# Columns of w1 read 36 apart, h laid out by nine transposes, and a finer last piece of wo in a decode kernel

## The chip, the cores and the metric

The kernel runs on one core of a Trainium2 chip. The metric is the device time of one execution in microseconds (us), as the median of several runs. The kernel before takes about 1295.3 us, and its fast runs lie between 1294.6 and 1297.3 us, so a difference of less than about 2 us means little in a single run.

The engines are TensorE (PE in the profile; PEld is its weight loads), VectorE (DVE), ScalarE (ACT), GpSimd (POOL) and SyncE (SP), which issues the loads here. The 16 DMA engines move data between HBM, the chip's main memory, and SBUF, the core's working memory.

A few words recur. A matmul takes two operands from SBUF: `lhsT`, loaded first as weights, and `rhs`, the *moving operand*; it writes to PSUM, TensorE's output memory. An *eviction* copies a result from PSUM to SBUF. A load is *issued* when SyncE puts it into the queue and *lands* when its completion is signalled. A *group* is, for the caches, one of 32 parts of K and V, and, in the up phase below, six matmuls that add up to one block of h. The *granted clock* is the share of full speed at which TensorE was allowed to run.

## The reference, cut to what matters

```python
B, D, H, Sk, Dh, F = 8, 576, 32, 4096, 128, 4608
def reference(...):
    x = A_x
    g = sigmoid((x * gate_w).sum(-1, keepdims=True))
    # A: one query per sequence against a cache of 4096 keys in each of 32 heads
    q = (x @ wq) -> [B, H, 1, Dh]
    a = softmax(q . k_cache * Dh**-0.5) @ v_cache -> @ wo
    # B: a small MLP on the layernormed x
    h = gelu(layernorm(x) @ w1 + b1)         # [8, 576] @ [576, 4608]
    b = h @ w2 + b2                          # [8, 4608] @ [4608, 576]
    return g * a + (1 - g) * b
```

The two caches are 2 x 8 x 32 x 4096 x 128 bf16 numbers, 537 MB. All weights together are 20 MB. All of it is read once.

## The kernel before

SBUF holds three big slots of 64 KB per partition. All loads of weights and caches are issued by SyncE into one queue, in a fixed order, each into the slot of the load three places earlier: wq, w1 and w2 first, then K of group 0 (called k0), k1, v0, k2, v1, k3 and so on over 32 groups. A load of 8.4 MB may be issued only when its slot is free. So k1 waits for the last matmul that reads w1, v0 for the last one that reads w2, k2 until k0 is worked off, and v1 until k1 is worked off.

```python
free[0] = [p_Q]               # k0 waits for the last read of wq
...
free[1] = [p_up]              # k1 waits for the last "up" matmul (reads w1)
...
free[2] = [p_b2]              # v0 waits for the last "down" matmul (reads w2)
```

The up phase computes h in four quarters of F (index c), each on its own quarter of TensorE's output columns (PSUM partitions 32c and up), in three blocks of 384 columns (index k). A group of six matmuls makes one block of one quarter: five over the rows of w1, and a sixth of a single row that adds the bias.

```python
for k in range(3):
    for c in range(4):
        col = c * FC + k * FB                       # FC = 1152, FB = 384
        o = up_ps[32 * c:32 * c + B, k, 0:FB]
        for kt in range(NKT):                       # 5
            r = w1_sb[:, kt, col:col + FB] ...      # 384 neighbouring columns
            p_up = op("tensor", lambda e, ...: e.matmul(o, lhsT=yT_sb[:, yi, :], rhs=r, ...))
        p_up = op("tensor", lambda e, ...: e.matmul(
            o, lhsT=one1[:, :], rhs=b1_row[:, col:col + FB], start=False, stop=True))
... gelu on VectorE and ScalarE into hrow [4 quarters x 8, 1152] ...
for j in range(NJ):                                 # 36 transposes of 32 columns, 36 apart
    p_hT = op("tensor", lambda e, j=j: e.matmul(
        ht_ps[0:32, j, :, :], lhsT=hrow[0:QP, j::NJ], rhs=per_quarter, ...))
v_hT = [op("vector", lambda e, c=c: e.tensor_copy(  # four evictions
    out=hT_sb[32 * c:32 * c + 32, :, :], in_=ht_ps[0:32, :, c, :]), [p_hT]) for c in range(4)]
```

w2 lies in SBUF with rows 36p to 36p+35 on partition p, so the transposed h must have row 36p + j on partition p too. That is where the step of 36 comes from.

At the end wo arrives in three pieces of rows, 32 x 4 small matmuls add it in, four evictions fill `out_sb`, and one store writes the result.

## Time and profile before

| | before |
|---|---|
| median of 3 runs | 1295.32 us (1294.81 to 1297.27) |
| bytes moved | 557.16 MB at a mean of 431 GB/s |
| busy share of the big load queue | 99.6% |
| TensorE / VectorE busy | 57% / 63% |
| up phase (first up matmul to the issue of k1) | 27.3 to 43.0 us |

Part 2 of the page of the kernel before cuts the span into 40 slices of 32.3 us. PEclk is TensorE's granted clock in tenths, DMA the busy share of the DMA engines in tenths, GB/s what they moved.

```profile
PEclk8799898878898887898787899778888877888888
DMA  9999999999999999999999999999999999999998
GB/s 406 427 447 424 439 430 436 432 430 436 434 428 436 436 432 438 430 438 432 430 436 434 428 436 438 430 438 430 438 430 432 436 432 434 432 438 430 436 424 366
DMA packets 10591, 557.16 MB, mean 431 GB/s; under 512 B 1201, under 2 KB 1233, under 8 KB 1745
```

The DMA engines are busy from the first slice to the last at a nearly constant rate. The kernel is bound by its loads: an engine can only cost time if it makes the queue run empty.

The timeline of SyncE before shows when loads were issued (start us, length us, engine, line, what, count). Its first line here merges two loads: k0 at 20.62 and k1 at 42.96.

```profile
20.62 22.68 SPq L384 DMA_DIRECT2D SL<-in_A_k_cache_dram  x2
59.34 0.33 SPq L384 DMA_DIRECT2D SL<-in_A_v_cache_dram  x1
84.42 0.33 SPq L384 DMA_DIRECT2D SL<-in_A_k_cache_dram  x1
111.47 0.33 SPq L384 DMA_DIRECT2D SL<-in_A_v_cache_dram  x1
```

The records of the same trace give the landings: k0 59.8, k1 79.2, v0 98.6, k2 117.9, v1 137.3 us. With the queue full a load lands every 19.35 us.

The timeline of TensorE in the up phase (start, length, line, operation, output and inputs, shape, count), at full clock:

```profile
31.30 0.98 PE L515 MATMUL PS<-SL 128*8 128x384 bf16 x5
32.20 0.32 PE L518 MATMUL PS<-SL,one 1*8 1x384 bf16 x1
32.45 0.98 PE L515 MATMUL PS<-SL 128*8 128x384 bf16 x5
33.36 0.32 PE L518 MATMUL PS<-SL,one 1*8 1x384 bf16 x1
```

Groups of six follow each other every 1.15 us. The windows view sums the engines and gives the clock (columns: stretch, length, busy time and count of PE, PEld, DVE, ACT, POOL, then clock, DMA share, GB/s). The first two groups ran at half clock:

```profile
27.30:31.30 4.00, 3.96 (x13) 1.14 (x13) 0.00 (x0) 0.00 (x0) 0.00 (x0) 0.55 1.15 498
31.30:43.00 11.70, 11.63 (x61) 4.29 (x60) 0.03 (x1) 0.00 (x0) 0.00 (x0) 1.00 0.97 419
```

The transposes of h and their evictions, and the last 3 us of the kernel, in the timeline:

```profile
50.60 2.30 PE L535 MATMUL PS<-ident,SL 104*32 104x32 bf16 x36 [7.67 <-DVE SL L528]
52.94 1.89 DVE L538 CAST SL<-PS 32x288 bf16<-32x288 f32 x4 [2.39 <-PE PS L535]
...
1290.22 0.30 PE L544 MATMUL PS<-SL,OT 128*8 128x144 bf16 x8 [0.21 <-DMA SL<-in_A_wo_dram]
1290.57 0.57 ACT L761 CAST out_sb<-PS 8x144 bf16<-8x144 f32 x2 [5.70 <-PE PS L544]
1290.57 0.63 DVE L761 CAST out_sb<-PS 8x144 bf16<-8x144 f32 x2 [3.50 <-PE PS L544]
1291.23 0.37 SPq L326 DMA_DIRECT2D out_dram<-out_sb  x1
```

### The profile page before, as it was taken

The numbers are of one execution on the slowest core, as the hardware profiler recorded it, in microseconds if no ns is written. First come the engines' busy times: TensorE is split into PE (matmuls) and PEld (weight loads), VectorE is DVE, ScalarE is ACT, GpSimd is POOL, SyncE is SP. The second block draws the span as 40 slices with busy tenths as digits, with TensorE's granted clock in tenths as the row PEclk, the third lists the DMA queues.
The fourth block names the chain that finished last, engine by engine and source line by source line (L and its number), as shares of the span: only waits on it lengthen the run. The fifth ranks groups of instructions, "written<-read, shape, count | busy, mean of one in ns | idle before, by whom it ended". The sixth has DMA issues, their size and how long they took to land.

```text
span 1293.2 us, 11790 instructions
## 1 busy us (share of the span) xinstructions
PE 733.4 (57%) x4926; PEld 337.1 (26%) x4926; DVE 819.7 (63%) x873; ACT 161.0 (12%) x587; POOL 40.4 (3%) x60
## 2 busy tenths in 40 slices
PE   3666566555556555556555556555556555556646
PEld 1322223122223222223222223222223222223223
DVE  2387567665567665567665567765567765567762
ACT  1011110111110011110011110011111011111011
POOL 1001000000000000000000000000000000000000
PEclk8799898878898887898787899778888877888888
DMA  9999999999999999999999999999999999999998
GB/s 406 427 447 424 439 430 436 432 430 436 434 428 436 436 432 438 430 438 432 430 436 434 428 436 438 430 438 430 438 430 432 436 432 434 432 438 430 436 424 366
DMA packets 10591, 557.16 MB, mean 431 GB/s; under 512 B 1201, under 2 KB 1233, under 8 KB 1745
## 3 DMA queue, kind: packets, MB, share of 16 engines
q1 hardware_dynamic: 10528, 556.94, 99.6%
q8 instruction: 9, 0.15, 0.0%
q10 hardware_dynamic: 50, 0.04, 0.0%
q14 instruction: 4, 0.03, 0.0%
HBM read 556.96 MB, written 0.01 MB: 431 GB/s over the span
## 4 chain that ended last, share of the span: by engine, by line
DMA 54%; DVE 26%; PE 14%; ACT 5%; issue 1%; SPq 0%; ACTq 0%; DVEq 0%
DMA SL<-in_A_k_cache_dram 50%; DVE SL L580 20%; PE PS L585 7%; DVE s_sb L591 5%; ACT P L625 4%; PE PS L640 4%; DMA SL<-in_B_w_dram 2%; DMA SL<-in_A_wo_dram 2%; PE PS L515 1%; PE PS L656 1%; ACT O_sb L645 1%; PE PS L544 0%; PE PS L518 0%; PE PS L649 0%; PE PS L535 0%
## 5 line engine op out<-in xcount | busy, mean ns | idle before, releaser
L585 PE MATMUL PS<-SL,ident 128*128 128x512 bf16 x2048 | 547.7, 420 | 518.3 <-DVE SL L580 518.3
L580 DVE TENSOR_TENSOR SL<-SL,q_bc 128x4096 bf16<-128x4096 bf16 x256 | 582.0, 2284 | 313.6 <-DMA SL<-in_A_k_cache_dram 313.6
L585 PEld LDWEIGHTS PS<-SL,ident 128*128 128x128 bf16 x2048 | 199.0, 106 | 853.8 <-DVE SL L580 614.8
L591 DVE TENSOR_REDUCE s_sb<-PS 128x32 f32<-128x512 f32 x256 | 175.8, 687 | 90.4 <-PE PS L585 90.3
L625 ACT ACTIVATE P<-s_sb,hb 128x256 bf16<-128x256 f32 x256 | 126.2, 494 | 663.3 <-PE PS L640 645.5
L640 PE MATMUL PS<-SL,P 128*32 128x512 bf16 x2048 | 128.5, 389 | 0.0
L640 PEld LDWEIGHTS PS<-SL,P 128*32 128x32 bf16 x2048 | 96.4, 138 | 17.9 <-issue 3.1
L564 POOL TENSOR_SCALAR Qm<-Q,sel 128x256 bf16<-128x256 bf16 x33 | 33.7, 1020 | 896.6 <-ACT O_sb L645 845.2
L572 ACT ACTIVATE q_bc<-PS 128x128 bf16<-128x128 f32 x33 | 9.1, 277 | 407.4 <-PE PS L569 407.4
L625 ACT ACTIVATION_READ_ACCUMULATOR P<-s_sb,hb 128x1 f32 x256 | 47.7, 186 | 0.0
L656 PE MATMUL PS<-O_sb,selq 128*32 128x128 f32 x256 | 34.2, 278 | 0.7 <-ACT O_sb L645 0.7
L656 PEld LDWEIGHTS PS<-O_sb,selq 128*32 128x32 f32 x256 | 26.0, 113 | 1.4 <-ACT O_sb L645 1.2
L645 ACT ACTIVATE O_sb<-PS 128x512 f32<-128x512 f32 x32 | 18.4, 574 | 10.0 <-PE PS L640 10.0
L523 DVE COPY SL<-PS 104x1152 f32<-104x1152 f32 x1 | 1.4, 1357 | 28.7 <-PE PS L518 28.7
L515 PE MATMUL PS<-SL 128*8 128x384 bf16 x60 | 13.2, 356 | 6.8 <-DMA SL<-in_B_w_dram 6.8
L669 DVE SCALAR_TENSOR_TENSOR On<-PS,rz,dqm 32x128 f32<-32x128 f32 x32 | 10.9, 339 | 9.0 <-PE PS L656 7.9
L683 POOL TENSOR_TENSOR OT<-OTs,g 32x96 bf16<-32x96 f32 (+2 forms) x12 | 4.2, 347 | 320.3 <-DVE OTs L673 320.2
L610 DVE TENSOR_REDUCE mA<-s_sb 128x1 f32<-128x256 f32 x32 | 13.4, 420 | 1.1
L673 DVE TENSOR_REDUCE OTs<-On 32x32 f32<-32x128 f32 x32 | 12.1, 378 | 1.1
L649 PE MATMUL PS<-acc,hsel 128*32 128x8 f32 x64 | 7.4, 188 | 5.9 <-ACT O_sb L645 4.7
L663 DVE TENSOR_REDUCE zs<-PS 32x1 f32<-32x8 f32 x32 | 4.7, 147 | 8.2 <-PE PS L656 7.9
L649 PEld LDWEIGHTS PS<-acc,hsel 128*32 128x32 f32 x64 | 4.5, 110 | 19.5 <-issue 12.7
(82 smaller groups left out, 114.5 us busy)
## 6 DMA issues: line engine op xcount, KB each, us to landing
SL<-in_A_v_cache_dram SPq DMA_DIRECT2D x2, 4096.0 KB, 38.4
SL<-in_B_w_dram SPq DMA_DIRECT2D x1, 5184.0 KB, 37.7
SL<-in_B_w_dram SPq DMA_DIRECT2D x1, 4608.0 KB, 24.1
SL<-in_A_wq_dram SPq DMA_DIRECT2D x1, 4096.0 KB, 13.0
SL<-in_A_wo_dram SPq DMA_DIRECT2D x1, 3456.0 KB, 22.0
SL<-in_A_wo_dram SPq DMA_DIRECT2D x1, 864.0 KB, 23.7
SL<-in_B_w_dram SPq DMA_DIRECT2D x1, 576.0 KB, 25.0
SL<-in_A_wq_dram SPq DMA_DIRECT2D x1, 512.0 KB, 13.6
```

Of the source, the lines that this page charges most:

```text
L515: p_up = op("tensor", lambda e, o=o, r=r, kt=kt, yi=yi: e.matmul(o, lhsT=yT_sb[:, yi, :], rhs=r, start=(kt == 0), stop=False), [v_yT, *ld_ ...
L564: g_qm[g] = op("gpsimd", lambda e: e.tensor_scalar(out=Qm[:, :, :].rearrange("p k d -> p (k d)"), in0=Q4[:, 2 * hg * DH:(2 * hg + 2) * DH] ...
L580: v_mult[g, c] = op("vector", lambda e: e.tensor_tensor(out=part, in0=part, in1=qb, op=ALU.mult), [land["k", g], a_qb[g]], token="tensor" ...
L585: p_sum[g, c] = op("tensor", lambda e, r=r, n=n: e.matmul(tr_ps[par][:, :], lhsT=ident[:, :], rhs=r, start=(n == 0), stop=(n == NCH - 1)), ...
L591: v_red[g, c] = op("vector", lambda e: e.tensor_reduce(out=s_sb[:, c * CT:(c + 1) * CT], in_=tr_ps[par][:, :].rearrange("p (t c) -> p t c" ...
L610: t = op("vector", lambda e: e.tensor_reduce(out=mA[:, 0:1], in_=s_sb[:, :], axis=AX.X, op=ALU.max), [v_red[g, NCK - 1], c_mA], token=own)
L625: a_exp[g] = op("scalar", lambda e, h=h: e.activation(out=P[:, :, h, :], in_=s_sb[:, :].rearrange("p (s t) -> p s t", s=2), func=ACT.Exp, ...
L640: p_pv[g] = op("tensor", lambda e, o=o, lhsT=lhsT, rhs=rhs, tq=tq: e.matmul(o, lhsT=lhsT, rhs=rhs, start=(tq < 4), stop=(tq >= NTQ - 4)), ...
L645: a_ev[g] = op("scalar", lambda e: e.activation(out=O_sb[:].rearrange("p t d -> p (t d)"), in_=o_ps[:, :], func=ACT.Copy), [p_pv[g], p_z.g ...
L649: p_z[g] = op("tensor", lambda e: e.matmul(oz_ps[0:32, DH:DH + HB], lhsT=hsel[:, :], rhs=acc[:, place(g), :], start=True, stop=True), [a_e ...
L656: p_oz[g] = op("tensor", lambda e, tt=tt: e.matmul(oz_ps[0:32, 0:DH], lhsT=selq[:, tt, :], rhs=O_sb[:, tt, :], start=(tt == 0), stop=(tt = ...
L673: v_norm[g] = op("vector", lambda e: e.tensor_reduce(out=OTs[:, :, place(g + 2)], in_=On[:, :].rearrange("p (q j) -> p j q", q=NDQ), axis= ...
```

## The change

Its intent: if the up matmuls already take their columns 36 apart, h comes out in the order that the transposes want. Each transpose can then cover 128 columns in a row, nine do instead of 36, and one eviction does instead of four. The last row of wo arrives in two half-width pieces, so that half of the output can be evicted while the other half still arrives. One VectorE instruction leaves each softmax. Small copies at the start move from VectorE to ScalarE.

```diff
+    def columns(t, at):
+        return bass.AP(tensor=t.tensor, offset=t.offset + at, ap=[list(t.ap[0]), [1, 3], [NJ, 128]])
+
     for k in range(3):
         for c in range(4):
-            col = c * FC + k * FB
             o = up_ps[32 * c:32 * c + B, k, 0:FB]
+            at = c * NJQ + 3 * k
             for kt in range(NKT):
-                r = w1_sb[:, kt, col:col + FB] if kt < NKF else w1_t[...]
...
+                if kt < NKF:
+                    ks = [(w1_sb[:, kt, :], at, yT_sb[:, kt, :], o)]
+                else:                                     # the last rows: two matmuls of 192 columns
+                    ks = [(w1_t, at, yT_sb[:, NKF, :], 0), (w1_t, at, yT_sb[:, NKF + 1, :], 1)]
...
             p_up = op("tensor", lambda e, o=o, at=at: e.matmul(
-                o, lhsT=one1[:, :], rhs=b1_row[:, col:col + FB], start=False, stop=True), [ld_b1, c_one1])
+                o, lhsT=one1[:, :], rhs=columns(b1_row, at), start=False, stop=True), [ld_b1, c_one1])
...
-    for j in range(NJ):
-        p_hT = ... matmul(ht_ps[0:32, j, :, :], lhsT=hrow[0:QP, j::NJ], rhs=per_quarter, ...)
-    v_hT = [... tensor_copy(out=hT_sb[32 * c:32 * c + 32, :, :], in_=ht_ps[0:32, :, c, :]) ... for c in range(4)]
+    for i in range(NJQ):                                  # NJQ = 9
+        p_hT = ... matmul(ht_ps[:, i, :, :], lhsT=hrow[0:QP, i, :], rhs=per_quarter, ...)
+    v_hT = [... tensor_copy(out=hT_sb.rearrange("p (c i) b -> p i c b", c=4), in_=ht_ps)]
...  (softmax: the negation goes into the instruction that makes hb8; one tensor_scalar less)
-    WO = ((0, 24), (24, 30), (30, 32))
+    WO = ((0, 24, 0, 4), (24, 31, 0, 4), (31, 32, 2, 4), (31, 32, 0, 2))
...
+        for i in range(4) if j < NJO - 1 else (2, 3, 0, 1):
...  (each eviction waits for its own quarter alone; VectorE and ScalarE take turns)
```

More of the change, by code (lines that the diff above doesn't have):

```diff
@@ L36 @@
 FC = F // 4
+NJQ = NJ // 4
 FB = FC // 3
@@ L265, in bass_gated_mix__mha_block_cached__mixer_channel_mlp__decode_kernel @@
     b1_row = late.take([1, F])
-    hrow = late.take([128, FC])
+    hrow = late.take([128, NJ // 4, 128])
     hT_sb = late.take([128, NJ, B])
@@ L276, in bass_gated_mix__mha_block_cached__mixer_channel_mlp__decode_kernel @@
     zs = sb("zs", [32, 1], F32)
+    rz = sb("rz", [32, 1], F32)
     acc = sb("acc", [128, GL, HB], F32)
@@ L292, in bass_gated_mix__mha_block_cached__mixer_channel_mlp__decode_kernel @@
     ident = sb("ident", [128, 128], BF16)
-    hneg = sb("hneg", [128, HB], F32)
+    hpos = sb("hpos", [128, HB], F32)
     sel32 = sb("sel32", [128, HB, TQ], F32)
@@ L298, in bass_gated_mix__mha_block_cached__mixer_channel_mlp__decode_kernel @@
     mB = sb("mB", [128, 32], F32)
-    mC = sb("mC", [128, 32], F32)
     mD = sb("mD", [128, 32], F32)
@@ L304, in bass_gated_mix__mha_block_cached__mixer_channel_mlp__decode_kernel @@
     O_sb = sb("O_sb", [128, TQ, DH], F32)
-    rz = sb("rz", [128, 1], F32)
     PS = nc.alloc_psum_tensor("PS", [128, 8 * 512], F32)
@@ L317, in bass_gated_mix__mha_block_cached__mixer_channel_mlp__decode_kernel @@
     g32_ps = bank[3][0:32, 64:64 + 2 * B]
-    ht_ps = PS[:, 0:NJ * 32].rearrange("p (j c b) -> p j c b", j=NJ, c=4)
+    ht_ps = PS[:, 0:NJ * B].rearrange("p (i c b) -> p i c b", i=NJQ, c=4)
     xt_ps = bank[7]
@@ L405, in bass_gated_mix__mha_block_cached__mixer_channel_mlp__decode_kernel @@
                                                     base=PH - 1, pattern=[[PH, HB], [0, NDQ]], channel_multiplier=-1), [t])
-    c_hneg = op("vector", lambda e: e.tensor_scalar(out=hneg[:, :], in0=hsel[:, ::NDQ], scalar1=-1.0, scalar2=60000.0,
+    c_hpos = op("vector", lambda e: e.tensor_scalar(out=hpos[:, :], in0=hsel[:, ::NDQ], scalar1=-1.0, scalar2=-60000.0,
                                                     op0=ALU.add, op1=ALU.mult), [c_hsel])
@@ L416, in bass_gated_mix__mha_block_cached__mixer_channel_mlp__decode_kernel @@
         axis=AX.X, op=ALU.add), [c_id])
-    c_selq = op("vector", lambda e: e.tensor_copy(
+    c_selq = op("scalar", lambda e: e.copy(
         out=selq[:].rearrange("p t (h q) -> p t h q", q=NDQ),
@@ L422, in bass_gated_mix__mha_block_cached__mixer_channel_mlp__decode_kernel @@
     c_b2 = op("gpsimd", lambda e: e.tensor_copy(out=b2_f, in_=b2_8), [ld_b2])
-    c_sp8 = op("vector", lambda e: e.tensor_copy(
+    c_sp8 = op("scalar", lambda e: e.copy(
         out=spread8[:].rearrange("b (c r) -> b c r", c=4),
@@ L427, in bass_gated_mix__mha_block_cached__mixer_channel_mlp__decode_kernel @@
         out=Rows[:], in_=ident[:, :].rearrange("p (h r) -> p h r", h=4), axis=AX.X, op=ALU.add), [c_id])
-    c_Sel = op("vector", lambda e: e.tensor_copy(
+    c_Sel = op("scalar", lambda e: e.copy(
         out=Sel[:].rearrange("p (h r) -> p h r", h=4),
@@ L465, in untransposed @@
     def untransposed(dst, col, waits):
-        return op("vector", lambda e: e.tensor_copy(
+        return op("scalar", lambda e: e.copy(
             out=dst.rearrange("p k b -> p (k b)"), in_=xt_ps[:, col:col + (NKF + 2) * B]), waits)
@@ L486, in bass_gated_mix__mha_block_cached__mixer_channel_mlp__decode_kernel @@
                                         start=True, stop=True), [c_one8])
-    v_g4 = op("vector", lambda e: e.tensor_copy(out=g4[:, :], in_=g4_ps), [t])
-    v_g32 = op("vector", lambda e: e.tensor_copy(out=g32[:].rearrange("p s b -> p (s b)"), in_=g32_ps), [t])
+    v_g4 = op("scalar", lambda e: e.copy(out=g4[:, :], in_=g4_ps), [t])
+    v_g32 = op("scalar", lambda e: e.copy(out=g32[:].rearrange("p s b -> p (s b)"), in_=g32_ps), [t])
     a_Q = []
@@ L505, in bass_gated_mix__mha_block_cached__mixer_channel_mlp__decode_kernel @@
     load_kv("k", 0)
+    def columns(t, at):
+        return bass.AP(tensor=t.tensor, offset=t.offset + at, ap=[list(t.ap[0]), [1, 3], [NJ, 128]])
     for k in range(3):
         for c in range(4):
-            col = c * FC + k * FB
             o = up_ps[32 * c:32 * c + B, k, 0:FB]
+            at = c * NJQ + 3 * k
             for kt in range(NKT):
-                r = w1_sb[:, kt, col:col + FB] if kt < NKF else w1_t[:, col - (c // 2) * (F // 2):][:, 0:FB]
-                yi = kt if kt < NKF else NKF + c // 2
-                p_up = op("tensor", lambda e, o=o, r=r, kt=kt, yi=yi: e.matmul(
-                    o, lhsT=yT_sb[:, yi, :], rhs=r, start=(kt == 0), stop=False),
-                    [v_yT, *ld_w1, *c_ps] if c == kt == k == 0 else ())
-            p_up = op("tensor", lambda e, o=o, col=col: e.matmul(
-                o, lhsT=one1[:, :], rhs=b1_row[:, col:col + FB], start=False, stop=True), [ld_b1, c_one1])
+                if kt < NKF:
+                    ks = [(w1_sb[:, kt, :], at, yT_sb[:, kt, :], o)]
+                else:
+                    ks = [(w1_t, at, yT_sb[:, NKF, :], 0), (w1_t, at, yT_sb[:, NKF + 1, :], 1)]
+                for w, col, lhsT, half in ks:
+                    rhs = columns(w, col)
+                    out_to = o
+                    if kt == NKF:
+                        rhs = bass.AP(tensor=rhs.tensor, offset=rhs.offset, ap=[rhs.ap[0], [1, 3], [NJ, 64]])
+                        out_to = o.rearrange("b (i p) -> b i p", i=3)[:, :, 64 * half:64 * half + 64]
+                    p_up = op("tensor", lambda e, o=out_to, r=rhs, lhsT=lhsT, kt=kt: e.matmul(
+                        o, lhsT=lhsT, rhs=r, start=(kt == 0), stop=False),
+                        [v_yT, *ld_w1, *c_ps] if c == kt == k == 0 else ())
+            p_up = op("tensor", lambda e, o=o, at=at: e.matmul(
+                o, lhsT=one1[:, :], rhs=columns(b1_row, at), start=False, stop=True), [ld_b1, c_one1])
     free[1] = [p_up]
@@ L528, in bass_gated_mix__mha_block_cached__mixer_channel_mlp__decode_kernel @@
     v_h = op("vector", lambda e: e.scalar_tensor_tensor(
-        out=hrow[0:QP, :].rearrange("p (k n) -> p k n", k=3), in0=h, scalar=g4[0:QP, 1:2], in1=t3,
+        out=hrow[0:QP, :, :].rearrange("p (k i) n -> p k (i n)", k=3), in0=h, scalar=g4[0:QP, 1:2], in1=t3,
         op0=ALU.mult, op1=ALU.mult), [t, v_g4])
@@ L533, in bass_gated_mix__mha_block_cached__mixer_channel_mlp__decode_kernel @@
     per_quarter = bass.AP(tensor=ident, offset=0, ap=[[pstride(ident), QP], [32, 4], [1, B]])
-    for j in range(NJ):
-        p_hT = op("tensor", lambda e, j=j: e.matmul(
-            ht_ps[0:32, j, :, :], lhsT=hrow[0:QP, j::NJ], rhs=per_quarter, start=True, stop=True),
-            [*v_hrow, *a_Q] if j == 0 else ())
-    v_hT = [op("vector", lambda e, c=c: e.tensor_copy(
-        out=hT_sb[32 * c:32 * c + 32, :, :], in_=ht_ps[0:32, :, c, :]), [p_hT]) for c in range(4)]
+    for i in range(NJQ):
+        p_hT = op("tensor", lambda e, i=i: e.matmul(
+            ht_ps[:, i, :, :], lhsT=hrow[0:QP, i, :], rhs=per_quarter, start=True, stop=True),
+            [*v_hrow, *a_Q] if i == 0 else ())
+    v_hT = [op("vector", lambda e: e.tensor_copy(
+        out=hT_sb.rearrange("p (c i) b -> p i c b", c=4), in_=ht_ps), [p_hT])]
     def quarters(lhsT, w, first, stop, waits):
@@ L615, in softmax @@
         gmb = bass.AP(tensor=gm, offset=0, ap=[[pstride(gm), 128], [1, 2], [0, PH]])
-        t = op("vector", lambda e: e.tensor_scalar(out=mC[:, :].rearrange("p (k r) -> p k r", k=2), in0=gmb,
-                                                   scalar1=-1.0, scalar2=None, op0=ALU.mult), [t], token=own)
-        t = op("vector", lambda e: e.transpose(mD[:, :], mC[:, :]), [t], token=own)
-        v_nm[g] = op("vector", lambda e: e.tensor_scalar(out=hb8[:, :], in0=hneg[:, :], scalar1=mD[:, 0:1], scalar2=None,
-                                                         op0=ALU.add), [t, c_hneg, a_exp.get(g - 1)],
+        t = op("vector", lambda e: e.transpose(mD[:, :], gmb), [t], token=own)
+        v_nm[g] = op("vector", lambda e: e.tensor_scalar(out=hb8[:, :], in0=hpos[:, :], scalar1=mD[:, 0:1], scalar2=-1.0,
+                                                         op0=ALU.add, op1=ALU.mult), [t, c_hpos, a_exp.get(g - 1)],
                      token="scalar" if in_loop(g) else None)
@@ L711, in load_wo @@
         w = A_wo.rearrange("(p j) n -> p j n", j=NJO)
-        for n, (j0, j1) in enumerate(WO):
-            t = load("sync", wo_sb[:, j0:j1, :], w[:, j0:j1, :], f"ld_wo{n}", waits)
-            ld_wo.update({j: t for j in range(j0, j1)})
+        for n, (j0, j1, i0, i1) in enumerate(WO):
+            cols = slice(i0 * QN, i1 * QN)
+            t = load("sync", wo_sb[:, j0:j1, cols], w[:, j0:j1, cols], f"ld_wo{n}", waits)
+            ld_wo.update({(j, i): t for j in range(j0, j1) for i in range(i0, i1)})
     for g in range(NG):
@@ L758, in bass_gated_mix__mha_block_cached__mixer_channel_mlp__decode_kernel @@
     place_o("vector", last - 1, last + 1)
+    p_a = {}
     for j in range(NJO):
-        p_a = quarters(OT[:, j, :], wo_sb[:, j, :], False, j == NJO - 1, [ld_wo[j], *g_ot.values()])
-    parts = [op("vector" if i < 2 else "scalar", lambda e, i=i: (e.tensor_copy if i < 2 else e.copy)(
-        out_sb[:, i * QN:(i + 1) * QN], y_ps[32 * i:32 * i + B, 0:QN]), [p_a]) for i in range(4)]
+        for i in range(4) if j < NJO - 1 else (2, 3, 0, 1):
+            p_a[i] = op("tensor", lambda e, i=i, j=j: e.matmul(
+                y_ps[32 * i:32 * i + B, 0:QN], lhsT=OT[:, j, :], rhs=wo_sb[:, j, i * QN:(i + 1) * QN], start=False,
+                stop=(j == NJO - 1)), [ld_wo[j, i], *g_ot.values()])
+    parts = [op("vector" if i % 2 == 0 else "scalar", lambda e, i=i: (e.tensor_copy if i % 2 == 0 else e.copy)(
+        out_sb[:, i * QN:(i + 1) * QN], y_ps[32 * i:32 * i + B, 0:QN]), [p_a[i]]) for i in (2, 3, 0, 1)]
     ld_out = [load("sync", out_flat, out_sb[:, :], "ld_out", parts)]
```

## The prediction

> **What bounds the kernel now.** The page shows 557.16 MB moved at a mean of 431 GB/s, with the DMA engines 99.6% busy on one queue; TensorE is 57% and VectorE 63% busy. The Trainium skill ("DMA: Bandwidth & Descriptors", Specifications) gives a fabric ceiling of 435 GB/s; the slices of this trace stand at 424 to 447 GB/s between the first and the last, so it agrees. The change moves no fewer bytes. So only three places can change the time: the start of the first load, a moment when the load queue runs empty, and the tail after the last weights land.
>
> **Start.** The timeline has the first big load issued at 0.79 us, before any changed instruction. Moving copies to ScalarE gains nothing: TensorE waits for wq (until 15 us) and w1 (until 27.3 us).
>
> **Tail.** In the timeline the last piece of wo lands at 1290.2, eight matmuls take 0.30 us, two evictions in a row on each of two engines about 0.6 us, and the store goes out at 1291.23. After it, the last half piece has two matmuls and one eviction per engine: I estimate 0.3 to 0.4 us saved. The two half rows are 576-byte runs and there is one transfer more; that may give back 0.1 to 0.3 us. Net -0.2 us.
>
> **Softmax.** One VectorE instruction (pitch 0.22 us) leaves each of 32 groups. It is covered: VectorE idles 313.6 us waiting for K (groups table). Worth 0.
>
> **h and its transposes.** 36 transposes (2.30 us) and four evictions (1.89 us) become nine and one; estimate 3.4 us less before v0 and everything behind it. But the moving operand of the up matmuls now steps 36 elements, 72 bytes. The skill ("SBUF — State Buffer", the note on SBUF cachelines) says each access that crosses to a new 16-byte line pays a penalty; no matmul of this trace has such a moving operand, so no run here shows its size. Now the up phase takes 15.6 us (27.3 to 42.93), about 1.15 us per group of six matmuls of 384 columns at full clock. If each column takes twice as long, it grows by some 10 us (12 groups x 0.96 us of streaming, the first two partly hidden by the half clock).
>
> **What of it reaches the queue.** Issue times and landings: k1 is issued at 43, its turn comes near 57; v0 at 59.3, turn near 76; k2 at 84.4, turn near 95; v1 at 111.47, while VectorE gets k2 only at 117.9. v1 is tightest: about 4 to 6 us, less a start latency near 1.4 us, plus the 3.4 us (and 0.2 of softmax) saved. So growth of the up phase to about 7 us is free; beyond, each us makes the queue run empty once, before v1, and is lost for good. Twice per column: 3 us lost. No penalty: 0. Four times: 20 to 25 us.
>
> **Prediction: 1298 us, range 1293.8 to 1309.** Faster by over 2%: 0.01; within 2%: 0.94; slower by over 2%: 0.05.
>
> **What would show it right.** Up matmuls still begin near 27.3 us; the up phase ends near 53 us rather than 43; from its end to v0's issue some 13 us rather than 16.4; v1 is issued some 6 us later (near 117 to 118); a dip in the DMA rate near 115 to 120 us, none elsewhere; from group 3 on VectorE again waits for K; store issued about 0.7 us rather than 1.0 us after the last landing.
>
> **What would make it wrong.** A stride that costs nothing (then about 1295 us, nearly neutral); a penalty of three or more times (k1 too comes late, 1305 us and up); half-row pieces of wo that land much later than two whole rows.

## The result, and the profile after

| | before | after |
|---|---|---|
| median | 1295.27 us (6 runs) | 1327.28 us (6 runs, 1326.67 to 1328.51) |
| ratio | | 1.0245, 95% interval 1.0232 to 1.0258 |
| up phase | 27.3 to 43.0 us | 27.0 to 81.0 us |
| up phase's end to the issue of v0 | 16.4 us | 12.8 us |

The kernel became slower by 32 us, outside the predicted range.

Part 2 of the page after; a slice is 33.1 us:

```profile
PEclk8559978988878898887889887788888778888878
DMA  9759899999999999999999999999999999999998
GB/s 404 314 222 440 351 440 418 438 441 427 435 435 435 427 435 439 423 435 441 423 435 441 431 431 435 435 427 435 438 425 435 443 421 437 439 429 433 435 422 362
```

Three slices carry the loss: the second (314 GB/s), the third (222) and the fifth (351). From the sixth on, the rates are those of before. In the second and third slice the clock stands at half. The windows view of the kernel after puts times to the gaps:

```profile
31.50:54.00 22.50, 22.50 (x37) 3.04 (x37) 0.00 (x0) 0.00 (x0) 0.00 (x0) 0.50 1.02 442
56.00:81.00 25.00, 24.96 (x40) 3.29 (x38) 0.00 (x0) 0.00 (x0) 0.00 (x0) 0.50 0.01 3
140.00:146.00 6.00, 4.20 (x25) 1.65 (x28) 4.61 (x5) 0.00 (x0) 0.00 (x0) 1.00 0.03 11
```

For 25 us (56 to 81) practically nothing is loaded (3 GB/s) while TensorE is 100% busy at half clock, and for another 6 us (140 to 146) again (11 GB/s). While the queue still had work, the strided reads did not hinder it: 442 GB/s from 31.5 to 54 us. SyncE's timeline says which loads were late (its first line again merges k0 and k1, k1 at 80.99):

```profile
20.28 61.04 SPq L384 DMA_DIRECT2D SL<-in_A_k_cache_dram  x2
93.75 0.33 SPq L384 DMA_DIRECT2D SL<-in_A_v_cache_dram  x1
119.26 0.33 SPq L384 DMA_DIRECT2D SL<-in_A_k_cache_dram  x1
145.80 0.33 SPq L384 DMA_DIRECT2D SL<-in_A_v_cache_dram  x1
```

k1 is the first, because it waits for the last read of w1. v1 is the second, because it waits for k1 to be worked off. Both were issued onto an empty queue: k1 landed 23.1 us after its issue (104.10), v1 also 23.1 us after (168.88). From this the slack in the kernel before can be worked out. v1 landed there at 137.27, so it could have been issued as late as 137.27 - 23.1 = 114.2 without harm, and was issued at 111.47: 2.7 us of slack. In the kernel after it was issued 34.3 us later than before. 34.3 - 2.7 = 31.6 us, and v1 did land 31.6 us later. That is the whole loss. The 2.7 us is not sharp: the runs below put this slack at 1.3 to 3.9 us.

The up matmuls themselves, after, in TensorE's timeline:

```profile
30.70 0.87 PE L530 MATMUL PS<-SL,one 1*8 1x384 bf16 x1
31.50 3.76 PE L527 MATMUL PS<-SL 128*8 128x384 bf16 x6
35.18 0.87 PE L530 MATMUL PS<-SL,one 1*8 1x384 bf16 x1
```

A group now takes 4.49 us instead of 1.15. The single records of the trace show a matmul of 384 columns starting every 0.720 us, where the kernel before had 0.163 us at full clock and 0.320 us at half clock.

The transposes and the tail after:

```profile
88.63 0.42 PE L547 MATMUL PS<-ident,SL 104*128 104x32 bf16 x9 [7.67 <-DVE SL L540]
89.10 0.46 DVE L550 CAST SL<-PS 128x288 bf16<-128x288 f32 x1 [0.52 <-PE PS L547]
...
1321.44 0.67 PE L773 MATMUL PS<-SL,OT 128*8 128x144 bf16 x32 [0.76 <-DMA SL<-in_A_wo_dram]
1322.15 0.63 DVE L776 CAST out_sb<-PS 8x144 bf16<-8x144 f32 x2 [3.88 <-PE PS L773]
1322.18 0.57 ACT L776 CAST out_sb<-PS 8x144 bf16<-8x144 f32 x2 [6.12 <-PE PS L773]
1322.84 0.37 SPq L326 DMA_DIRECT2D out_dram<-out_sb  x1
```

The transposes gained what they were meant to gain (2.30 to 0.42 us, evictions 1.89 to 0.46 us). The tail gained nothing: the last 32 matmuls run as one stream and the evictions follow two by two, as before.

### The profile page after: what moved, and what is told of

Its sections match the earlier page's. It is cut to its first block, busy times and chain, and to the rows that moved or that the text cites. A ratio compares the mean times of both kernels' runs of the same rounds, so it can differ in the third digit from the quotient of the medians.

```text
span 1324.9 us, 11728 instructions
## 1 busy us (share of the span) xinstructions
PE 769.4 (58%) x4911; PEld 336.0 (25%) x4911; DVE 811.5 (61%) x831; ACT 163.5 (12%) x595; POOL 37.2 (3%) x60
## 4 chain that ended last, share of the span: by engine, by line
DMA 52%; DVE 25%; PE 17%; ACT 5%; issue 1%; SPq 0%; ACTq 0%; DVEq 0%
DMA SL<-in_A_k_cache_dram 48%; DVE SL L592 20%; PE PS L597 7%; DVE s_sb L603 5%; ACT P L635 4%; PE PS L650 4%; PE PS L527 3%; DMA SL<-in_B_w_dram 2%; DMA SL<-in_A_wo_dram 2%; PE PS L666 1%; PE PS L530 1%; ACT O_sb L655 1%; PE PS L556 0%; PE PS L659 0%; SPq L326 0%
## 5 line engine op out<-in xcount | busy, mean ns | idle before, releaser
L576 POOL TENSOR_SCALAR Qm<-Q,sel 128x256 bf16<-128x256 bf16 x33 | 30.4, 922 | 934.9 <-ACT O_sb L655 847.3
L527 PE MATMUL PS<-SL 128*8 128x384 bf16 (+1 forms) x72 | 45.1, 778 | 6.8 <-DMA SL<-in_B_w_dram 6.8
L527 PEld LDWEIGHTS PS<-SL 128*8 128x8 bf16 x72 | 6.3, 100 | 45.0 <-issue 45.0
L530 PE MATMUL PS<-SL,one 1*8 1x384 bf16 x12 | 10.5, 872 | 0.0
## 6 DMA issues: line engine op xcount, KB each, us to landing
SL<-in_A_wo_dram SPq DMA_DIRECT2D x1, 3456.0 KB, 21.9
SL<-in_A_wq_dram SPq DMA_DIRECT2D x1, 512.0 KB, 13.3
```

Source lines behind the costliest of these rows:

```text
L527: p_up = op("tensor", lambda e, o=out_to, r=rhs, lhsT=lhsT, kt=kt: e.matmul(o, lhsT=lhsT, rhs=r, start=(kt == 0), stop=False), [v_yT, *ld_ ...
L530: p_up = op("tensor", lambda e, o=o, at=at: e.matmul(o, lhsT=one1[:, :], rhs=columns(b1_row, at), start=False, stop=True), [ld_b1, c_one1])
L576: g_qm[g] = op("gpsimd", lambda e: e.tensor_scalar(out=Qm[:, :, :].rearrange("p k d -> p (k d)"), in0=Q4[:, 2 * hg * DH:(2 * hg + 2) * DH] ...
```

## The experiments

The theory was that the strided moving operand is the whole loss, by way of the load queue. Rivals: another part of the change costs something; the strided reads hinder the DMA writes themselves; or half of the loss is the half clock that TensorE was granted. All twelve runs are told here. Each is compared with runs of the kernel before on the same chip.

### Everything but the stride

The kernel after with w1 contiguous again, and so with the 36 transposes and four evictions of before.

```diff
-                    ks = [(w1_sb[:, kt, :], at, yT_sb[:, kt, :], o)]      # and the rest of the strided loop
+                r = w1_sb[:, kt, col:col + FB] if kt < NKF else w1_t[...]  # the loop of before
```

> The kernel after with w1 read in contiguous columns again, and so with the 36 transposes and four evictions of before; softmax, ScalarE copies and wo pieces stay as changed. Theory (the strided moving operand is the whole loss): 1294.8 to 1295.5 us, up phase 15.6 us, no gap in the DMA rate. Rival (the copies on ScalarE or the half-row pieces of wo cost something): some of the 32 us stays, over 1298 us.

Measured: 1295.98 us (before 1296.11 on that chip), ratio 1.0006, interval 0.9989 to 1.0022. The softmax, the copies on ScalarE and the pieces of wo cost nothing and gain nothing that shows (the interval leaves room for about 2 us).

### The stride alone

The kernel before with only the strided up matmuls and the nine transposes.

```diff
-                r = w1_sb[:, kt, col:col + FB] if kt < NKF else w1_t[...]
+                    ks = [(w1_sb[:, kt, :], at, yT_sb[:, kt, :], o)]      # and the rest of the strided loop
```

> The kernel before with only w1's columns taken 36 apart and the nine transposes. Theory: 1327 to 1328 us, up phase 53.9 us, queue empty before k1 (about 25 us) and again before v1 (about 6 us). Rival: clearly less than 1327 us, the rest being made by the other parts.

Measured: 1328.27 us, ratio 1.0251, interval 1.0234 to 1.0268, with the same two gaps in the windows view:

```profile
56.00:81.00 25.00, 25.00 (x40) 3.29 (x38) 0.00 (x0) 0.00 (x0) 0.00 (x0) 0.50 0.01 3
140.00:147.00 7.00, 5.20 (x24) 1.94 (x22) 5.87 (x5) 0.00 (x0) 0.00 (x0) 1.00 0.11 47
```

These two runs place the loss in the stride.

### A longer up phase without a stride

The groups of the kernel before, contiguous, some of them done twice. The result stays correct.

```diff
-    for k in range(3):
-        for c in range(4):
+    for n_g in range(12 + 12):          # and 12 + 4 in the other run
+            k, c = divmod(n_g % 12, 4)
```

> The kernel before with its twelve groups of up matmuls done twice (contiguous, same result), so the up phase is 13.9 us longer with nothing else changed. Theory (only the length of the up phase counts, and v1's slack in the kernel before is near 2.7 us, read back from the 32 us lost): 11 us lost, 1306 us, all at v1 or k1. Rival A (the queue has slack to spare up to 7 us or more): 1302 us or less. Rival B (the strided reads also hinder the DMA writes directly): then this run loses less than its length tells while the strided one loses more.

> The kernel before with four of its groups of up matmuls done twice: up phase 4.6 us longer. Theory (v1's slack in the kernel before is near 2.7 us): 1.5 to 2.5 us lost, 1297 us. Rival (slack of 4 to 6 us as I had read it): nothing lost, 1295.3 us.

Measured for twelve more: 1305.76 us (1305.39 to 1306.06), ratio 1.0077. k1 was issued 13.8 us later than in the kernel before, v1 13.8 us later (125.27). 13.8 less the slack of 2.7 is 11.1 us; v1 landed 10.9 us later, and the median is 9.7 to 10.5 us higher, depending on whether it is set against the chip's own runs of before or against 1295.3. So the length of the up phase alone predicts the loss, and no hindrance of the DMA by strided reads is needed.

Four more gave 1299.73 us, with a wide spread (1297.33 to 1301.24), more than expected. The windows view of the profiled run shows why:

```profile
35.00:39.00 4.00, 4.00 (x13) 1.12 (x12) 0.00 (x0) 0.00 (x0) 0.00 (x0) 0.50 1.34 571
39.00:43.00 4.00, 4.00 (x22) 1.38 (x21) 0.00 (x0) 0.00 (x0) 0.00 (x0) 0.99 0.72 311
```

In this execution the clock stayed at half until about 39 us, not until 31, so the up phase was 8.2 us longer, not 4.6. v1 was issued 8.2 us later and landed 4.3 us later, so the slack here was 3.9 us and not 2.7: v1 landed 21.9 us after its issue, although its queue was empty (4 GB/s from 116 to 120 us, and the issue at 119.67). Why it landed sooner than the 23.1 us of the kernel after isn't known. The rival, no loss at all, is out, but this run measures the slack only roughly.

### Clock or time: strided and contiguous groups mixed

The kernel before; each of the twelve groups reads w1 by its own pattern. Its output is wrong, which doesn't matter for the time. In this and the next two runs the sixth matmul is one more of 128 rows in place of the one-row bias matmul, so that all six are alike.

```diff
+    PATTERNS = [C, C, C, C, S, C, C, S, S, C, C, S]        # C: [[1, 384]]   S: [[36, 384]]
+    for n_g, pat in enumerate(PATTERNS):
+        k, c = divmod(n_g % 12, 4)
+        for kt in range(NKT + 1):
+            r = bass.AP(tensor=SL, offset=SLOT + 16 * kt, ap=[[pstride(SL), 128], *pat])
+            p_up = ... matmul(o, lhsT=yT_sb[:, kt, :], rhs=r, start=(kt == 0), stop=(kt == NKT))
```

> Wrong result on purpose. The kernel before; its twelve groups of six matmuls of 384 columns read w1 contiguous (C) or stepping 36 elements (S), in the order C C C C S C C S S C C S. Theory 1 (the read is bound by time, not by TensorE's clock): an S group takes 4.5 us even right after C groups at full clock, 1.95 ns per column. Theory 2 (2.34 cycles per column of the granted clock, and the half clock of the run after doubled it): the first S group at full clock takes about 2.3 us. Total: up phase 27 us by theory 1 and about 20 us by theory 2, so 1304 or 1297 us.

Measured: 1294.94 us, ratio 0.9996. No time was lost, against both theories: the up phase took only 13.3 us in spite of four strided groups. The clock was full, as the windows view shows:

```profile
33.00:34.00 1.00, 1.00 (x6) 0.29 (x4) 0.00 (x0) 0.00 (x0) 0.00 (x0) 1.00 1.47 622
34.00:35.00 1.00, 1.00 (x6) 0.22 (x3) 0.00 (x0) 0.00 (x0) 0.00 (x0) 1.00 0.19 83
```

The single records of that stretch. The eighth group (column group 3) is on the left; on the right are the end of the fifth and, from 33.939, the start of the ninth (both column group 0):

```
start us   modelled length us     start us   modelled length us
32.434     0.902                  32.497     0.902
33.155     0.902                  33.218     0.902
33.875     0.902                  33.939     0.902
34.596     0.902                  34.660     0.902
```

There are two streams, one per column group. In each, a matmul starts every 0.72 us, as in the kernel after at half clock. Two things follow. The strided read is bound by time, not by the granted clock: theory 1 holds for the single stream. And **two strided streams on different column groups don't slow each other**: both keep 0.72 us. That was in no theory of mine, and it is why the totals missed.

### Which steps cost

The same kernel with another list of patterns: steps 36, 24, 16, 12, 9, 8, 7, 6, 4, 3, 2, 1.

```diff
+    PATTERNS = [[[36, 384]], [[24, 384]], [[16, 384]], [[12, 384]], [[9, 384]], [[8, 384]], [[7, 384]], ..., [[1, 384]]]
```

> Wrong result on purpose. The kernel before; its twelve groups of six matmuls of 384 columns step 36, 24, 16, 12, 9, 8, 7, 6, 4, 3, 2, 1 elements of 2 bytes. Theory (the cost comes from each element lying in a new 16-byte line): full cost 4.5 us a group down to step 8, less from 7, near the contiguous 1.15 us (2.0 at half clock) at step 4 and below. Rival (any step over 1 costs the same): 4.5 us down to step 2.

Measured: 1294.71 us, ratio 0.9996; again streams overlap and no time is lost. The lengths of the records (each about 0.17 us longer than the distance from one start to the next) sort by step:

| step (elements) | 1 and 2 | 3 | 4 | 6 | 7 | 8 | 9 to 36 |
|---|---|---|---|---|---|---|---|
| 16-byte lines per 384 columns | 48, 96 | 144 | 192 | 288 | 336 | 384 | 384 |
| length of one matmul, us | 0.33 | 0.42 | 0.52 | 0.69 | 0.77 | 0.85 to 0.89 | 0.87 to 0.90 |

From step 3 to step 7 each element of step adds about 0.088 us ((0.77 - 0.42) / 4) and 48 lines: 1.8 ns per line. Beyond step 8 the length no longer grows, as the count of lines no longer does. The rival (any step costs the same) is out. The Trainium skill, in the note on SBUF cachelines of "SBUF — State Buffer", gives the line as 16 bytes; the knee at step 8 agrees with that. It also says that one can stride up to 8 bf16 elements for free; for this operand at full clock only a step of 2 was free.

### Runs of neighbouring columns

> Wrong result on purpose. The kernel before; its groups read 384 columns in runs: step 36 with runs of 1, 2, 4, 8, 16; step 40 (whole 16-byte lines) with runs of 2, 4, 8; step 40 alone; step 40 with runs of 16; step 36 with runs of 32; contiguous. Theory (cost per line touched): halves with each doubling of the run until the contiguous time is reached, near runs of 4; step 40 no slower than 36. Rival (cost per change of step or of pattern): runs of 2 cost as much as runs of 1.

```diff
+    PATTERNS = [[[36, 384]], [[36, 192], [1, 2]], [[36, 96], [1, 4]], [[36, 48], [1, 8]], ..., [[40, 384]], ..., [[1, 384]]]
```

Measured: 1294.98 us, ratio 0.9996. Step 36 with runs of two: a matmul every 0.36 us, half of 0.72, so the rival (cost per change of pattern) is out. Runs of four, eight and sixteen at step 36 ran mostly at half clock and took about the 0.32 us of a contiguous matmul there. Step 40 missed the expectation: alone it needs 0.80 us per matmul, 11% more than step 36. Why isn't settled here.

### Who kept the streams apart: the bias matmuls moved last

In the kernel after, no two groups overlapped; in the probes they did. What the probes lack is the one-row bias matmul after each group. So in the kernel after only that was moved, with every strided read kept:

```diff
             ...
-            p_up = ... matmul(o, lhsT=one1[:, :], rhs=columns(b1_row, at), start=False, stop=True)
+    for k in range(3):
+        for c in range(4):
+            o = up_ps[32 * c:32 * c + B, k, 0:FB]
+            p_up = ... matmul(o, lhsT=one1[:, :], rhs=columns(b1_row, c * NJQ + 3 * k), start=False, stop=True)
```

> The kernel after, with only its twelve one-row bias matmuls moved behind all the others; every strided read stays. In the probes, strided matmuls of neighbouring column groups ran two or three at a time, each still 0.72 us. Theory 3 (a strided stream is slow by itself, but streams of different column groups overlap, and the one-row matmul after each group kept them apart): up phase 16 to 22 us instead of 53.9, queue never empty, 1295 to 1297 us. Rival (the probes overlapped for another reason, such as reading the same columns, and the strided reads share one port's time): up phase stays over 45 us and the time over 1318 us.

Measured: 1297.05 us (1296.09 to 1298.05), ratio 1.0015, interval 1.0000 to 1.0030. The correct result, 30 us faster than the kernel after. TensorE's timeline:

```profile
27.11 19.42 PE L527 MATMUL PS<-SL 128*8 128x384 bf16 x72 [8.08 <-DMA SL<-in_B_w_dram]
46.46 2.33 PE L533 MATMUL PS<-SL,one 1*8 1x384 bf16 x12
```

The up phase took 21.7 us instead of 54.0. v1 was issued at 114.28, right at the limit of 114.2 worked out above, and yet landed 1.5 us late, at 138.81 instead of 137.27. So the slack was only 1.3 us in this execution, and the expectation that the queue would never run short was missed by that much.

### The four quarters innermost

As before, and the loop order changed so that four neighbours in the program belong to four column groups:

```diff
     for k in range(3):
-        for c in range(4):
-            ...
-            for kt in range(NKT):
+        for kt in range(NKT):
+            for c in range(4):
```

> As the run with the bias matmuls last, and the loop over the four column groups innermost, so that four strided streams can run at once from the first. Theory 3: up phase 14 to 18 us, 1295 us. Rival (no more than two or three at a time): no shorter than with the bias last alone.

Measured: 1295.52 us (1295.34 to 1296.50), ratio 1.0005, interval 0.9989 to 1.0020: the loss is gone, with every column of w1 still read 36 apart. TensorE's timeline, and the view by source line (length min/median/max in ns) for the strided matmuls:

```profile
27.11 10.98 PE L527 MATMUL PS<-SL 128*8 128x384 bf16 x72 [7.65 <-DMA SL<-in_B_w_dram]
38.02 2.33 PE L533 MATMUL PS<-SL,one 1*8 1x384 bf16 x12
...
L527 PE MATMUL PS<-SL x72: 540/901/908, 27.1 to 37.6; 128*8 128x384 bf16 x48, 128*8 128x192 bf16 x24
```

Each matmul is as long as in the kernel after (901 ns against 892 in its view by line), but four run at a time: four start within 0.02 us, the next four 0.72 us later. The up phase is 13.3 us, shorter than before the change. The Trainium skill says under "TensorE: Matmul & The Clock Gate", Part 3 (The mechanism), that matmuls on different tiles of the array overlap; these four column groups agree. No run here shows why a one-row matmul stops the overlap when it stands between groups. In the probes a sixth matmul of 128 rows in its place did not, so it is something of that matmul, its single row or its operands; twelve one-row matmuls in a row overlap each other (2.33 us for all twelve, where one alone holds its stream for about 0.7).

### The same reorder in the kernel before

```diff
-            p_up = ... matmul(o, lhsT=one1[:, :], rhs=b1_row[:, col:col + FB], start=False, stop=True)
+    for k in range(3):
+        for c in range(4):                  # the same matmuls, after all others
```

> The kernel before with its bias matmuls moved behind all the others, w1 contiguous. Theory 3: the up phase shrinks from 15.6 to 9 to 12 us, because contiguous matmuls of neighbouring column groups overlap too; the time stays at 1295 us, since the load queue was never empty. Rival (overlap only fills the gaps of strided reads): up phase 14 us or more.

Measured: 1295.09 us, ratio 0.9999. The up phase shrinks from 15.6 to 6.0 us (most of it at half clock), further than expected, and the time does not move, as the queue was never empty.

```profile
27.13 5.38 PE L515 MATMUL PS<-SL 128*8 128x384 bf16 x60 [7.72 <-DMA SL<-in_B_w_dram]
32.45 0.66 PE L521 MATMUL PS<-SL,one 1*8 1x384 bf16 x12
```

### Nine transposes without a strided w1

The stride can also be moved to where it is cheap. If partition p holds four runs of nine rows of w2 instead of one run of 36, w1 stays contiguous and only the nine weight loads of the transposes step 9 elements.

```diff
-    ld_w2 = load("sync", w2_sb, B_w2.rearrange("(p j) n -> p j n", j=NJ), "ld_w2")
+    ld_w2 = load("sync", w2_sb.rearrange("p (c i) n -> p c i n", c=4),
+                 B_w2.rearrange("(c p i) n -> p c i n", c=4, i=NJQ), "ld_w2")
...
-            ht_ps[:, i, :, :], lhsT=hrow[0:QP, i, :], rhs=per_quarter, ...
+            ht_ps[:, i, :, :], lhsT=hrow[0:QP, i::NJQ], rhs=per_quarter, ...
```

> The kernel after, but w1 contiguous and the nine transposes kept, by loading w2 in another grouping of its rows (each partition gets four runs of nine rows) and letting the weight load of each transpose step 9 elements. Theory: the stride is cheap on nine weight loads; 1294.5 to 1295.5 us, v0 issued near 56 us. Rival: the four shorter runs per partition or the strided weight loads cost time, over 1297 us.

Measured: 1295.59 us, ratio 0.9999, interval 0.9982 to 1.0016; the nine transposes take 0.73 us with the strided weight loads, against 0.42 us in the kernel after. v0 was issued at 58.91 and not near 56 as expected: the clock stayed at half until 37.1 us in the profiled execution, so the up phase ended at 45.7. It is as good as the kernel before, but not better.

```profile
53.37 0.73 PE L535 MATMUL PS<-ident,SL 104*128 104x32 bf16 x9 [7.67 <-DVE SL L528]
```

### An attempt to beat both

The regrouped w2, the bias last, and the last two rows of wo (not one) in two half-width pieces behind a piece of six rows.

```diff
-    WO = ((0, 24, 0, 4), (24, 31, 0, 4), (31, 32, 2, 4), (31, 32, 0, 2))
+    WO = ((0, 24, 0, 4), (24, 30, 0, 4), (30, 32, 2, 4), (30, 32, 0, 2))
```

> The version with the regrouped w2, bias matmuls last, and the last two rows of wo (not one) in two half-width pieces behind a piece of six rows. Meant to beat both: the store should go out about 0.6 to 0.8 us after the last piece lands, against 1.05 us before, so 1295.0 us or 0.3 us less than before, which 5 rounds will hardly resolve. Rival (small pieces land later by as much): no difference in the distance from the last V landing to the store, 12.1 us in both kernels.

Measured over 5 rounds: 1295.57 us, ratio 1.0003, interval 0.9989 to 1.0016. No gain. The last piece landed at 1290.18, but TensorE started its last ten matmuls only at 1290.66; what it waited for in between, the profile doesn't show. The store went out 1.56 us after that landing, not 0.6 to 0.8. From the landing of the last V to the issue of the store it took 12.7 us, against 12.1 in the kernels before and after; but that distance says little in one execution, since in the three probes, whose tail is that of the kernel before, it was 12.0, 12.3 and 12.8 us. No version tried beats the kernel before, and none had much to gain: the load queue is full in all the good ones.

## Why the prediction was wrong

- *What bounds the kernel, and where a change can count*: right. The loss is made of moments in which the load queue was empty, and of nothing else.
- *Start*: right. The first load is issued at 0.79 us in both.
- *Softmax worth 0, copies worth 0*: right as far as the noise lets one see (everything but the stride: 1.0006, interval 0.9989 to 1.0022).
- *3.4 us less for the transposes and their evictions*: right in size. From the end of the up phase to v0's issue it was 16.4 us and became 12.8, 3.6 us less.
- *Slack of v1*: right. The prediction said growth of the up phase "to about 7 us is free". From the landings: 2.7 us of slack (1.3 to 3.9 in other runs), plus 3.6 for the transposes and 0.2 for the softmax, 6.5 us. The start latency that it took as near 1.4 us measured 1.0 us, from an issue onto an empty queue to the first packet (80.99 to 81.96 us, and 145.80 to 146.75).
- *"Twice per column: 3 us lost"*: **this term failed.** The step of 36 cost 0.720 us per matmul of 384 columns where the contiguous one takes 0.163 us at full clock: 4.4 times, not twice. The up phase grew by 38 us (15.6 to 54.0), not by 10. I had taken a factor of two for a penalty of which the skill gives no size; the probes give about 1.8 to 1.9 ns per 16-byte line, whatever the clock. With 38 us in place of 10, and its 7 us of free growth, the prediction's own arithmetic gives 31 us, and the measured loss is 32.0. So the path to the loss was right, and this one size was wrong.
- *"Four times: 20 to 25 us"*: the text's own numbers should have given more: three extra times 0.96 us, times 12 groups, is 35 us, or 33 with the first two groups at half clock before; less 7 that is 26 to 28 us. Even the 20 to 25 us would have meant 1315 to 1320 us. So the range was drawn too narrow at the top even for the case that was named.
- *What the factor hides*: the cost of the stride was full only because the matmuls ran one after the other. Had I looked at the single records before, I would have seen that no two groups of the up phase overlapped although each block of four groups lies on four different column groups. With the order changed, the same stride costs nothing (1.0005).
- *Up phase from 27.3 to near 53, v1 near 117 to 118, one dip near 115 to 120*: wrong in consequence; it ended at 81, v1 came at 145.8, and the dips were at 56 to 81 and at 140 to 146. That a larger penalty would make k1 late as well was said, and happened.
- *Tail -0.2 us, store 0.7 us after the last landing*: wrong, though too small to matter. The store went out 1.04 us after the last landing (1.05 before). The three last pieces landed within 0.4 us of each other (1321.40, 1321.60, 1321.80), so there was nothing left to overlap.

## What to carry to other kernels

When a layout change moves a stride into the moving operand of a matmul, count the 16-byte lines it touches, not the columns: here a line cost 1.8 to 2.1 ns, so the steps of 8 to 36 bf16 elements cost 4.2 to 4.4 times the contiguous read at full clock, and a step of 40 cost 4.9 times. If the matmuls use only a few output columns, put neighbours in the program on different column groups and keep one-row bias matmuls out from between them: four strided streams then ran in the time of one. In a kernel bound by its loads, work out the slack of each load from landings and issues (landing, less the time a load needs on an empty queue, less the issue) before deciding that a slower phase is free, and leave some margin: that time was 21.9 to 23.2 us here.

## What the Trainium skill lacked or had wrong

- "SBUF — State Buffer", the note on SBUF cachelines: it says that 8 bf16 elements of stride are free and gives no size for the penalty. For the moving operand of a matmul at full clock, a step of 2 was free, a step of 4 took 0.52 us against 0.33 (record length), and a step of 8 took 0.85 to 0.89. The cost was about 1.8 ns per 16-byte line (1.9 at step 36), the same at half and at full clock (0.72 us per 384 lines in both).
- No page that I read has it: four strided streams on four column groups run at once, each at its own 0.72 us, so the penalty is per stream, not shared (up phase 13.3 us interleaved with the bias matmuls last, against 54.0 us one by one).
- "TensorE: Matmul & The Clock Gate", Part 3: it gives no size for what a one-row matmul between groups costs. Moving twelve of them to the end shortened the up phase from 15.6 to 6.0 us with contiguous columns, and from 54.0 to 21.7 us with strided ones. The skill is not silent on what may lie behind it: see "TensorEngine Tiling (Array Packing)", Key Properties, on changes of the tiling mode. It has no size there either, and no run here tests whether that is the reason.
- "TensorE: Matmul & The Clock Gate", Part 1: "the default state is throttled, and activity releases the throttle." Here 54 us of serial strided matmuls, with PE shown 100% busy, never released it (granted clock 0.50 from 24.0 to 92.3 us), while two strided streams at once did (bias matmuls last: full clock from 31.1 us), and four did too (0.94 on average from 31.0 to 40.3 us). So the busy share of PE in the profile does not tell by itself whether the clock is released.
- No page has it: a step of 80 bytes was 11% slower per matmul than one of 72 bytes (0.80 against 0.72 us). Unexplained.
